# Recurrence with feed-forward on one core: another layout for a, another place for its decay, and a new order

## The chip, the cores and the metric

The kernel runs on one core of one Trainium2 chip. The metric is device time in microseconds. A run of the kernel before took 263.14 us in the median of three (261.58, 263.14, 263.40).

## The reference, cut to what matters

Four batches of eight heads run a recurrence over 768 steps with a 40 x 40 state each. Its output, as 3,072 tokens of 320 features, goes through a feed-forward layer with 2,048 hidden units and a squared relu.

```
for t in range(S):
    y[:, :, t] = einsum('bhd,bhde->bhe', rt, state)
    Sa = einsum('bhde,bhe->bhd', state, at)
    state = state * wt[:, :, None, :] - einsum('bhd,bhe->bhde', Sa, bt) \
            + einsum('bhd,bhe->bhde', vt, kt)
...
h = x @ w_in;  g = maximum(h, 0) ** 2;  out = g @ w_out
```

## The kernel before, in words

The 768 steps are cut into twelve chunks of 64. Within a chunk the recurrence is written as matrix products: w's running products G (the decay from the chunk's start, "the gate") scale k and b by 1/G and a by G, two triangular 64 x 64 products per head stand in for the steps inside the chunk, and a state STb is handed from chunk to chunk. Heads are packed in pairs (two times 40 features in 128 rows, padded to 64) and batches in two halves g of the array's rows, so most matmuls run in a part of the TensorE array: row-tiled (64 x 128), column-tiled (128 x 64), or both (64 x 64). The feed-forward and the sums over steps with UTX run on the whole array.

`load(c)` issues the six inputs of chunk c on SP's queue, two DMAs each. w, k, b, a and v are laid with the step on the partition, so each piece of memory that is read is one head's 40 features of one step, 160 bytes. r alone is laid in eight-step rows: a partition holds eight steps of a head pair's member, 320 values, 1,280 bytes in a piece (`rv`, line 409). An output store has 1,280-byte rows too. Weights go over POOL's queue: WIN in four parts of 256 KB, WOUT in four of 320 KB, WLAST (the last 64 of the 320 input features) in two DMAs of 128 KB.

`prep(c)` makes the chunk's operands. ln of w; hi and lo (its bfloat16 split); ci (matmuls with UTI, inclusive sums of ln w over the steps, for k and b) and ei (exp of minus that, iG); cx (matmuls with UTX, exclusive sums) and ex (exp, Gex); cg (16 matmuls with SEL that have two columns each, line 462: the chunk's whole decay, with the feature on the partition) and eg (exp, gL). mulKB multiplies k and b by iG in two halves; mulA multiplies a by Gex; castR and castV make bfloat16 of r and v. TK, TA and TR are transposes on TensorE into PSUM; tK, tA and tR copy them out (lines 350 and 355 are the copies of VectorE and ScalarE), a's and r's into the two halves of AR. EN is the first triangle (mask mEN, line 556).

`rec(c)` runs AS, EV, NU (with u0 and u1), and S with s, which multiplies the new state by gL while it leaves PSUM (line 648). `read(c)` runs TV, the second triangle CX, RS and Y, y and yd (times Gex, line 718) and the transposes XT. `ffn(c)` works in four quarters u of the hidden units: F (eight whole-array matmuls with WIN, features 0 to 255), FL (four row-tiled ones with WLAST, features 256 to 319, into the same PSUM pair), f (relu, line 772), q (the square, in place, on VectorE line 778 or GpSimd line 780), then O (eight matmuls with WOUT per quarter) and o, the copy out, and st, the store on SP.

PSUM is used as four tiles of a pair of banks; the digit behind PE in the order says which. The order of the instructions of all engines together is written out by hand as one text, ORDER (line 87), whose entries say engine, operation, chunk and part; each engine runs its own entries in that order. A planner's costs (`c_act`, `c_dve`, `pe`) stand in the code, but only ORDER decides. Buffers of raw inputs have two turns, of gates three (NG), of KB and VU three.

Of the kernel before, what the change touches and what calls it, by code (L numbers as in the profile page):

```python
# [91 lines left out]
castV 0 g0; POOL castV 0 g1; PE2 TR 0; DVE mEN 0 g1; ACT tR 0 g0; ACT ex 1; DVE hi 2; PE0 EV 0; SP
ldr 1; DVE lo 2; ACT u0 0; PE3 cx 2; PE NU 0; PE cg 2; ACT u1 0 g0; SP ldv 1; ACT tR 0 g1; DVE
mulKB 1 h0; POOL mulKB 1 h1; ACT u1 0 g1; PE2 S 0 g0; SP ldw 3; ACT ex 2; PE S 0 g1; ACT eg 2; DVE
s 0 q1; PE0 TK 1; POOL mulA 1; DVE s 0 q0; SP ldb 2; ACT castR 1; POOL win3; PE3 TA 1; ACT tK 1;
PE2 TV 0; DVE tA 1; DVE tV 0; PE3 ci 2 h1; SP ldv 2; ACT castV 1 g0; PE0 EN 1 g0; PE2 EN 1 g1; ACT
eg 1; DVE mEN 1 g0; ACT ei 2 h1; PE1 ci 2 h0; ACT ei 2 h0; PE3 CX 0 g1; DVE mEN 1 g1; POOL castV 1
g1; PE0 AS 1; ACT ln 3; POOL win1; PE EV 1; DVE hi 3; DVE mCX 0 g1; PE1 CX 0 g0; ACT u0 1; SP ldk
2; PE2 TR 1; ACT tR 1 g1; PE NU 1; DVE mCX 0 g0; ACT u1 1 g0; DVE tR 1 g0; PE3 Y 0; ACT u1 1 g1;
POOL lo 3; PE1 TS 0; DVE y 0; PE2 TV 1; ACT tS 0; DVE yd 0; PE0 SC 1; DVE tV 1; PE S 1 g0; SP lda  # L100
2; PE3 XT 0; POOL castV 2 g1; PE1 CX 1 g0; PE2 CX 1 g1; DVE xt 0; POOL castV 2 g0; PE S 1 g1; DVE
mCX 1 g0; PE3 RS 1; POOL wlast; SP ldr 3; DVE mCX 1 g1; PE1 cx 3; DVE s 1 q0; PE Y 1; POOL win0;
PE2 ci 3 h0; DVE mulKB 2 h1; PE cg 3; DVE yd 1; DVE y 1; ACT ex 3; SP ldr 2; ACT eg 3; DVE s 1 q1;
PE3 ci 3 h1; PE1 XT 1; ACT ei 3 h1; POOL win2; DVE xt 1; PE0 F 0 u3; DVE mulKB 2 h0; DVE mulA 2;
PE FL 0 u3; SP ldk 4; PE3 TS 1; PE1 TK 2; ACT castR 3; POOL wout0; DVE tK 2; ACT ei 3 h0; ACT f 0
u3; PE2 TR 3; PE1 F 0 u0; SP ldk 3; ACT tR 3 g0; ACT tR 3 g1; PE0 F 1 u0; ACT tS 1; PE FL 1 u0; PE
FL 0 u0; PE2 TA 2; ACT f 1 u0; POOL castR 2; PE3 F 0 u1; DVE tA 2; POOL wout2; ACT f 0 u0; PE0 EN
2 g0; PE2 F 0 u2; DVE mEN 2 g0; SP lda 3; PE FL 0 u2; PE FL 0 u1; DVE q 0 u0; PE1 EN 2 g1; ACT f 0
u2; PE0 F 1 u3; DVE mEN 2 g1; ACT f 0 u1; PE2 AS 2; PE EV 2; POOL wout1; PE FL 1 u3; ACT u0 2; PE1
TR 2; ACT f 1 u3; PE NU 2; PE3 F 1 u1; ACT tR 2 g0; SP ldb 3; DVE q 1 u3; ACT u1 2 g0; PE0 F 1 u2;  # L110
DVE q 0 u3; ACT tR 2 g1; DVE q 0 u2; ACT u1 2 g1; PE FL 1 u1; PE FL 1 u2; DVE q 0 u1; ACT f 1 u1;
PE1 TV 2; POOL wout3; DVE q 1 u0; PE2 O 0 u0; ACT f 1 u2; DVE tV 2; PE3 RS 2; SP ldw 4; DVE q 1
u2; PE0 CX 2 g0; PE1 CX 2 g1; DVE mCX 2 g0; DVE mCX 2 g1; PE O 0 u1; DVE mulA 3; DVE q 1 u1; PE O
0 u2; SP ldv 3; PE0 SC 2; PE S 2 g0; PE Y 2; PE S 2 g1; DVE y 2; PE1 O 1 u0; SP lda 4; DVE s 2 q0;
PE O 1 u1; DVE yd 2; DVE s 2 q1; PE O 0 u3; DVE mulKB 3 h1; SP ldb 4; DVE mulKB 3 h0; PE O 1 u2;
ACT o 0; ACT ln 4; PE3 XT 2; PE0 TA 3; ACT hi 4; PE2 TK 3; DVE xt 2; SP ldw 5; PE O 1 u3; DVE tK
3; POOL castV 3 g1; PE3 F 2 u0; POOL lo 4; DVE tA 3; ACT o 1; ACT castV 3 g0; PE2 EN 3 g1; SP st
0; PE0 EN 3 g0; PE FL 2 u0; DVE mEN 3 g1; PE1 F 2 u2; ACT f 2 u0; DVE mEN 3 g0; PE FL 2 u2; PE2 TS
2; ACT f 2 u2; PE3 AS 3; SP st 1; DVE tS 2; PE EV 3; DVE q 2 u0; PE0 ci 4 h0; ACT u0 3; PE1 ci 4
h1; SP ldv 4; PE2 SC 3; ACT ei 4 h0; PE NU 3; ACT ei 4 h1; PE0 cx 4; ACT u1 3 g0; SP ldr 4; DVE  # L120
mulKB 4 h1; PE cg 4; ACT u1 3 g1; DVE mulKB 4 h0; PE1 F 2 u1; ACT ex 4; ACT eg 4; PE FL 2 u1; ACT
ln 5; DVE mulA 4; PE S 3 g0; SP ldw 6; PE S 3 g1; ACT f 2 u1; POOL hi 5; PE3 TA 4; DVE s 3 q1; PE0
TK 4; POOL lo 5; PE1 TV 3; DVE tA 4; SP ldr 5; ACT tK 4; DVE s 3 q0; PE3 F 2 u3; DVE tV 3; PE2 ci
5 h0; POOL castV 4 g1; PE0 EN 4 g0; SP ldk 5; ACT ei 5 h0; PE FL 2 u3; DVE mEN 4 g0; PE1 EN 4 g1;
POOL castR 4; ACT f 2 u3; PE2 cx 5; SP ldb 5; POOL q 2 u1; PE cg 5; DVE mEN 4 g1; ACT castV 4 g0;
PE0 ci 5 h1; PE3 CX 3 g0; ACT ei 5 h1; PE1 AS 4; DVE mCX 3 g0; PE EV 4; ACT eg 5; ACT ex 5; SP lda
5; PE0 O 2 u0; ACT u0 4; DVE q 2 u2; PE NU 4; PE2 TR 4; ACT u1 4 g0; PE3 CX 3 g1; SP ldv 5; PE O 2
u1; DVE mCX 3 g1; ACT u1 4 g1; ACT tR 4 g0; PE1 RS 3; DVE tR 4 g1; ACT ln 6; PE3 SC 4; PE S 4 g0;
DVE q 2 u3; PE S 4 g1; ACT hi 6; SP ldw 7; PE Y 3; DVE s 4 q0; PE O 2 u2; POOL lo 6; DVE y 3; PE O
2 u3; DVE s 4 q1; POOL castR 5; SP ldb 6; DVE yd 3; DVE mulKB 5 h0; POOL mulKB 5 h1; PE2 XT 3; ACT  # L130
o 2; PE3 TR 5; PE1 TV 4; DVE xt 3; ACT tR 5 g1; PE0 ci 6 h0; DVE tV 4; PE2 F 3 u1; ACT ei 6 h0; SP
ldk 6; POOL mulA 5; ACT tR 5 g0; PE0 ci 6 h1; PE1 CX 4 g0; PE FL 3 u1; ACT ei 6 h1; DVE mCX 4 g0;
PE3 F 3 u3; ACT f 3 u1; PE0 TA 5; SP lda 6; PE1 TS 4; POOL q 3 u1; DVE tA 5; PE2 TS 3; DVE tS 4;
PE FL 3 u3; PE0 TK 5; ACT f 3 u3; DVE tS 3; PE1 F 3 u0; POOL castV 5 g1; SP st 2; DVE tK 5; PE FL
3 u0; PE3 CX 4 g1; ACT f 3 u0; PE2 F 3 u2; DVE mCX 4 g1; ACT ln 7; PE FL 3 u2; PE0 EN 5 g1; PE1 EN
5 g0; ACT f 3 u2; SP ldw 8; DVE mEN 5 g1; PE3 cx 6; PE cg 6; DVE mEN 5 g0; SP ldv 6; PE2 AS 5; ACT
eg 6; POOL hi 7; ACT castV 5 g0; PE0 RS 4; PE Y 4; DVE q 3 u0; POOL mulKB 6 h1; ACT ex 6; PE EV 5;
DVE y 4; PE1 O 3 u0; ACT u0 5; DVE mulKB 6 h0; SP lda 7; POOL mulA 6; PE NU 5; DVE yd 4; PE O 3
u1; DVE q 3 u2; ACT u1 5 g0; ACT u1 5 g1; PE3 TK 6; POOL lo 7; PE0 TA 6; PE2 TV 5; ACT tK 6; DVE
tA 6; PE O 3 u2; DVE tV 5; PE0 cx 7; ACT ln 8; DVE q 3 u3; PE3 CX 5 g1; PE2 XT 4; DVE mCX 5 g1; PE  # L140
O 3 u3; ACT xt 4; PE2 ci 7 h1; ACT o 3; PE3 EN 6 g1; PE cg 7; ACT ei 7 h1; DVE mEN 6 g1; SP st 3;
PE1 EN 6 g0; ACT eg 7; ACT ex 7; PE2 ci 7 h0; DVE mEN 6 g0; PE3 SC 5; SP ldk 7; ACT castV 6 g0; PE
S 5 g0; POOL mulA 7; PE S 5 g1; ACT ei 7 h0; PE0 CX 5 g0; PE1 F 4 u0; DVE mCX 5 g0; SP ldb 7; POOL
castV 6 g1; PE2 F 4 u3; DVE s 5 q0; POOL hi 8; SP ldr 7; PE FL 4 u3; DVE s 5 q1; PE FL 4 u0; POOL
lo 8; ACT f 4 u3; PE0 RS 5; PE Y 5; SP lda 8; PE3 AS 6; ACT f 4 u0; DVE yd 5; PE EV 6; DVE y 5;
PE2 TS 5; SP ldv 7; ACT u0 6; PE1 XT 5; DVE tS 5; PE0 F 4 u1; ACT xt 5; PE FL 4 u1; DVE mulKB 7
h0; POOL mulKB 7 h1; PE2 TA 7; ACT f 4 u1; PE NU 6; SP ldw 9; DVE tA 7; PE1 F 4 u2; ACT u1 6 g0;
DVE q 4 u1; ACT u1 6 g1; PE0 ci 8 h1; POOL castR 7; PE2 TK 7; ACT ei 8 h1; DVE q 4 u0; PE3 ci 8
h0; SP ldr 6; PE FL 4 u2; ACT ei 8 h0; PE0 F 5 u3; DVE tK 7; ACT f 4 u2; PE3 F 5 u0; DVE q 4 u2;
PE FL 5 u3; SP ldb 8; PE1 TV 6; ACT f 5 u3; POOL castV 7 g1; PE2 SC 6; DVE tV 6; PE S 6 g0; SP ldk  # L150
8; PE S 6 g1; POOL q 4 u3; PE0 EN 7 g0; PE FL 5 u0; DVE s 6 q0; PE1 cx 8; ACT f 5 u0; PE cg 8; DVE
mEN 7 g0; PE3 F 5 u2; SP ldb 9; ACT eg 8; ACT ex 8; DVE s 6 q1; POOL castR 6; ACT castV 7 g0; PE
FL 5 u2; PE0 EN 7 g1; POOL mulA 8; PE1 TR 7; ACT f 5 u2; DVE mEN 7 g1; PE2 O 4 u0; SP ldw 10; ACT
tR 7 g0; ACT tR 7 g1; PE3 TS 6; PE0 TR 6; PE1 AS 7; PE EV 7; PE O 4 u1; SP ldv 8; ACT u0 7; DVE
mulKB 8 h0; ACT ln 9; PE O 4 u2; ACT tR 6 g1; DVE tR 6 g0; POOL hi 9; DVE tS 6; POOL mulKB 8 h1;
PE NU 7; PE0 CX 6 g1; ACT u1 7 g0; PE3 CX 6 g0; PE O 4 u3; DVE mCX 6 g0; POOL lo 9; ACT u1 7 g1;
PE1 F 5 u1; DVE mCX 6 g1; ACT o 4; POOL q 5 u0; PE3 TA 8; SP st 4; PE FL 5 u1; PE2 ci 9 h1; DVE tA
# [723 lines left out]
```

## Time and profile before

| | us |
|---|---|
| median of three runs | 263.14 |
| the profiled execution's own time | 260.79 |
| its span, first to last instruction | 258.80 |
| TensorE matmul in flight | 226.8 |
| VectorE busy | 189.0 |
| ScalarE busy | 152.7 |
| GpSimd busy | 96.9 |

The profile is of one execution. A busy share is a mean over the span; stages with different limits are told apart by windows. Matmuls overlap, so their start-to-start distance, and not their mean duration, is what one costs in a dense stretch.

### The profile page before, as it was taken

Reading aid. Unit: us, or ns where it says so; the run is one execution under the profiler, and the core shown is the slowest. Engines: PE = TensorE matmul, PEld = TensorE weight load, DVE = VectorE, ACT = ScalarE, POOL = GpSimd, SP = SyncE. Lnnn points to the kernel's source line nnn. Section 1 sums busy time; section 2 is a strip of 40 time slices with the busy share of each in tenths; the row PEclk is TensorE's granted clock in tenths of the full one; section 3 lists DMA queues with packets and bytes.
Section 4 is the critical chain, followed back from the end, with each engine's and each line's share of the span. In section 5 each row is a group of like instructions: output and inputs, shape, how many; then the busy total and the mean of one; then the engine's idle time right before and its main releaser. Section 6 shows DMA issues by size and latency. Waiting matters only on the chain.

```text
span 258.8 us, 12193 instructions
## 1 busy us (share of the span) xinstructions
PE 226.8 (88%) x5608; PEld 175.3 (68%) x5608; DVE 189.0 (73%) x230; ACT 152.7 (59%) x203; POOL 96.9 (37%) x91
## 2 busy tenths in 40 slices
...
GB/s 110 191 167 175 133 151 159 215 152 165 131 144 179 167 134 148 167 147 7 61 185 144 154 131 149 178 171 151 198 135 4 5 3 54 56 3 3 51 23 78
DMA packets 135506, 30.92 MB, mean 119 GB/s; under 512 B 125728, under 2 KB 135456, under 8 KB 135456
## 3 DMA queue, kind: packets, MB, share of 16 engines
q1 hardware_dynamic: 131712, 27.54, 60.2%
q0 software_dynamic: 3744, 2.62, 7.2%
...
q14 instruction: 7, 0.06, 0.1%
...
## 4 chain that ended last, share of the span: by engine, by line
PE 56%; DVE 18%; DMA 7%; ACT 6%; SPq 6%; issue 4%; POOL 1%; DVEq 0%; ACTq 0%; POOLq 0%
PE pb L369 49%; PE pb L373 7%; DVE EN L556 4%; DMA raw_r<-in_r_dram 3%; DMA raw_w<-in_w_dram 2%; DVE CX L556 2%; DVE STb L648 2%; DMA raw_kb<-in_b_dram 1%; SPq L405 1%; ACT VU L355 1%; DVE AR L350 1%; DVE VUT L350 1%; DVE G L778 1%; SPq L392 1%; ACT AR L355 1%
## 5 line engine op out<-in xcount | busy, mean ns | idle before, releaser
L772 ACT ACTIVATE G<-pb 128x1024 bf16<-128x1024 f32 x46 | 46.1, 1022 | 24.1 <-PE pb L369 23.9
L369 PE MATMUL pb<-WOUT,G 128*128 128x320 bf16 x384 | 57.4, 300 | 0.5 <-DVE G L778 0.4
L369 PE MATMUL pb<-XT,WIN 128*128 128x256 bf16 x384 | 49.2, 276 | 2.2 <-DVE XT L350 1.2
L780 POOL TENSOR_TENSOR G<-G 128x1024 bf16<-128x1024 bf16 x16 | 30.6, 1919 | 42.4 <-ACT G L772 42.4
L369 PEld LDWEIGHTS <-G 128*128 128x128 bf16 x384 | 35.2, 98 | 14.9 <-issue 0.6
L369 PEld LDWEIGHTS <-WIN 128*128 128x128 bf16 x384 | 35.9, 98 | 8.8 <-issue 3.4
L778 DVE TENSOR_TENSOR G<-G 128x1024 bf16<-128x1024 bf16 x32 | 30.6, 975 | 8.7 <-ACT G L772 8.7
L556 DVE TENSOR_TENSOR CX<-pb,MSK 128x1024 bf16<-128x1024 f32 x24 | 28.8, 1219 | 6.2 <-PE pb L369 5.7
L556 DVE TENSOR_TENSOR EN<-pb,MSK 128x1024 bf16<-128x1024 f32 x24 | 28.6, 1217 | 3.2 <-PE pb L369 3.2
L365 DVE TENSOR_TENSOR KB<-raw_kb,iG 128x640 bf16<-128x640 f32 x15 | 14.2, 960 | 11.1 <-ACT iG L444 4.9
L355 ACT ACTIVATE osb<-pb 128x640 f32<-128x640 f32 x12 | 8.5, 704 | 22.9 <-PE pb L369 22.9
L648 DVE TENSOR_TENSOR STb<-pb,gL 64x640 bf16<-64x640 f32 x22 | 18.0, 818 | 4.8 <-PE pb L369 4.4
L355 ACT ACTIVATE VU<-pb 64x640 bf16<-64x640 f32 x23 | 16.0, 697 | 8.4 <-PE pb L369 6.1
L363 POOL TENSOR_TENSOR KB<-raw_kb,iG 128x640 bf16<-128x640 f32 x9 | 15.1, 1681 | 15.5 <-ACT iG L444 5.8
L359 POOL CAST VU<-raw_v 64x640 bf16<-64x640 f32 x14 | 10.0, 721 | 28.6 <-DMA raw_v<-in_v_dram 28.5
L444 ACT ACTIVATE iG<-pb 128x640 f32<-128x640 f32 x24 | 16.4, 702 | 6.7 <-PE pb L369 2.2
L363 POOL TENSOR_TENSOR lo<-lnW,hi 128x640 bf16<-128x640 f32 x8 | 11.7, 1468 | 22.1 <-DMA raw_v<-in_v_dram 7.1
L369 PEld LDWEIGHTS <-EN 64*64 64x64 bf16 x768 | 15.2, 113 | 6.7 <-issue 4.4
L369 PE MATMUL pb<-XT,WLAST 64*128 64x256 bf16 x192 | 17.6, 274 | 0.0
L350 DVE COPY AR<-pb 128x1024 bf16<-128x1024 bf16 (+1 forms) x17 | 11.7, 687 | 6.4 <-PE pb L373 4.0
L355 ACT ACTIVATE AR<-pb 128x512 bf16<-128x512 bf16 x19 | 11.0, 595 | 7.6 <-PE pb L373 7.5
L718 DVE TENSOR_TENSOR Yb<-pb,Gex 128x640 bf16<-128x640 f32 (+1 forms) x24 | 12.6, 549 | 3.1 <-PE pb L369 3.0
...
## 6 DMA issues: line engine op xcount, KB each, us to landing
...
```

The costliest lines, as they stand in the source:

```text
L350: lambda: nc.vector.tensor_copy(out=o_(), in_=i_())))
L355: alts.append(("ACT", c_act(n), lambda: nc.scalar.activation(out=o_(), in_=i_(), func=ACTF.Copy, scale=1.0 if scale is None else scale)))
L363: return [("POOL", 40 + 2.35 * n, lambda: nc.gpsimd.tensor_tensor(out=o_(), in0=a_(), in1=b_(), op=op)), ("DVE", c_dve(n), lambda: nc.vect ...
L365: ("DVE", c_dve(n), lambda: nc.vector.tensor_tensor(out=o_(), in0=a_(), in1=b_(), op=op))]
L369: return lambda: nc.tensor.matmul(out=o_(), lhsT=l_(), rhs=r_(), start=start, stop=stop, skip_group_check=True)
L373: return lambda: nc.tensor.transpose(out=o_(), in_=i_(), identity=IDb[rows(g), :])
L444: ew(f"ei {c} h{jh}", [("ACT", c_act(2 * n), lambda hb=hb, jh=jh: nc.scalar.activation(out=iG[0][:].rearrange("p (g j) e -> p g (j e)", g= ...
L556: evac(f"m{nm} {c} g{g}", lambda s, n: [("DVE", c_dve(n), lambda: nc.vector.tensor_tensor(out=dst[q2][:, g, s].rearrange("p q i t -> p (q ...
L648: ew(f"s {c} q{q}", [("DVE", c_dve(2 * n), lambda q=q: nc.vector.tensor_tensor(out=STb[q2][rows(q), :, q, 0:D], in0=slot(hs, FP32)[rows(q) ...
L772: ("ACT", c_act(1024), lambda gb=gb, hf=hf: nc.scalar.activation(out=gb, in_=slot(hf, FP32)[:], func=ACTF.Relu)),
L778: ("DVE", 690, lambda gv=gv: nc.vector.tensor_tensor(out=gv, in0=gv, in1=gv, op=ALU.mult)),
L780: ("POOL", 1900, lambda gv=gv: nc.gpsimd.tensor_tensor(out=gv, in0=gv, in1=gv, op=ALU.mult))],
```

## The change

- a is loaded like r, in eight-step rows; raw_a has r's shape. castA (GpSimd or ScalarE) makes it bfloat16, and TA transposes it as TR does, without waiting for the gate.
- mulA, SEL, cg and eg are gone. cf, 32 row-tiled matmuls per chunk, makes the running sums of ln w with the feature on the partition; ef takes their exp into GT, 64 steps and a leading 1, 65 columns per head pair. tA, in two halves on VectorE, multiplies the transposed a by GT while it leaves PSUM; s takes the chunk's whole decay from GT's last column.
- Rings of gates (Gex, GT) have two turns, not three.
- In quarters 1 and 3 of the feed-forward FL comes first and opens the PSUM pair, F closes it.
- q can run on ScalarE (Square).
- ORDER is new throughout. By its count of entries: mulKB on GpSimd 18 instead of 9 of 24, hi and lo all twelve on GpSimd (7 and 8 before), castR all twelve on GpSimd (7 before), castV 19 instead of 14 of 24 there, castA 11 of 12 there; q 16 each on VectorE, ScalarE and GpSimd (32, 0, 16 before); relus on VectorE 10 instead of 2; u1 on VectorE 7 instead of 1, tR 10 instead of 5, tV 12 instead of 10, tK 7 instead of 8.

```diff
-ORDER = """SP ldw 0; SP ldw 1; SP ldk 0; SP ldb 0; ACT ln 0; POOL hi 0; DVE lo 0; SP ldr 0; PE0 cx 0; PE cg
-0; PE1 ci 0 h0; ACT ex 0; PE2 ci 0 h1; SP lda 0; ACT ei 0 h1; ACT ei 0 h0; SP ldw 2; ACT ln 1; ACT
-hi 1; ACT eg 0; DVE mulKB 0 h0; POOL lo 1; SP ldv 0; DVE mulKB 0 h1; POOL castR 0; SP ldb 1; PE3
...
+ORDER = """SP ldw 0; SP lda 0; SP ldk 0; SP ldb 0; ACT ln 0; SP ldw 1; POOL castA 0; POOL hi 0; PE0 TA 0;
+POOL lo 0; SP ldv 0; PE1 ci 0 h0; PE2 ci 0 h1; ACT ei 0 h0; PE3 cf 0; ACT ei 0 h1; SP ldb 1; PE1
+cx 0; ACT ef 0; DVE mulKB 0 h1; DVE mulKB 0 h0; DVE tA 0 g0; PE2 TK 0; SP lda 1; DVE tA 0 g1; ACT
...
-    raw_a = buf("raw_a", [128, NJ, D], FP32, NA)
+    raw_a = buf("raw_a", [128, 2, 8 * D], FP32, NA)
...
-    NG = 3
+    NG = 2
     Gex = buf("Gex", [128, NJ, D], FP32, NG)
-    gL = buf("gL", [128, NJ], FP32, NG)
+    GT = buf("GT", [128, NJ, L + 1], FP32, NG)
...
+    for x in GT:
+        nc.vector.memset(x[:, :, 0:1], 1.0)
...
+        for nm, x, ring in (("a", a, raw_a), ("r", r, raw_r)):
+            xv = x[:, :, t0, :].rearrange("b (p q) (k i) e -> q (b p) k (i e)", q=2, i=8)
+
+            def go(xv=xv, ring=ring):
+                for q in range(2):
+                    nc.sync.dma_start(out=ring[c % 2][:, q, :], in_=xv[q])
...
-        pe(f"cg {c}", "D", 2, ms, reads=[("hi",), ("lo",)], writes=[hx])
...
+        hf = ("A", "f", c)
+        ms = []
+        for p in range(NP):
+            for x in (h_, l_):
+                for g in range(2):
+                    ms.append(mm(
+                        lambda p=p, g=g: slot(hf, FP32)[:, g, L * p:L * p + L],
+                        lambda x=x, p=p, g=g: x[rows(g), 2 * p:2 * p + 2, :].rearrange(
+                            "p h e -> p (h e)"),
+                        lambda g=g: UTI[rows(g), 0:L], x is h_ and p == 0, x is l_))
+        pe(f"cf {c}", "R", L, ms, reads=[("hi",), ("lo",)], writes=[hf], alloc=[hf])
+        ew(f"ef {c}", [("ACT", c_act(1024), lambda: nc.scalar.activation(
+            out=GT[q3][:, :, 1:L + 1].rearrange("p (g m) t -> p g m t", g=2),
+            in_=slot(hf, FP32)[:].rearrange("p g (m t) -> p g m t", t=L), func=ACTF.Exp))],
+           reads=[hf], writes=[("GT", q3)], free=[hf])
...
-        ew(f"mulA {c}", mul_alts(lambda: tA[q2][:, :, 0:D], lambda: raw_a[c % NA][:],
-                                 lambda: Gex[q3][:], 640),
-           reads=[("raw", "a", c % NA), ("Gex", q3)], writes=[("tA", q2)])
...
-        ew(f"tA {c}", copy_alts(
-            lambda: AR[q2][:, 0].rearrange("p g j t -> p g (j t)"),
-            lambda: slot(ha, BF16)[:, :, 0:512], 1024, True),
-           reads=[ha], writes=[("AR", q2)], free=[ha])
...
+        for g in range(2):
+            ew(f"tA {c} g{g}", [("DVE", c_dve(512), lambda g=g: nc.vector.tensor_tensor(
+                out=steps(AR[q2][:, 0, g]), in0=turned(ha, g),
+                in1=steps(GT[q3][:, NP * g:NP * g + NP, 0:L]), op=ALU.mult))],
+               reads=[ha, ("GT", q3)], writes=[("AR", q2, g)], free=[ha])
...
-                    in1=gL[c % NG][rows(q), :].rearrange("p (j o) -> p j o", o=1).broadcast_to(
-                        [64, NJ, D]), op=ALU.mult))],
+                    in1=GT[c % NG][rows(q), :, L:L + 1].broadcast_to([64, NJ, D]),
+                    op=ALU.mult))],
...
+            tail = u % 2 == 1
...
+            for x in (1, 0) if tail else (0, 1):
+                if x:
+                    pe(f"FL {c} u{u}", "R", NT, ml, **last)
+                else:
+                    pe(f"F {c} u{u}", "D", NT, ms, **wide)
...
+                ("ACT", c_act(1024), lambda gv=gv: nc.scalar.activation(
+                    out=gv, in_=gv, func=ACTF.Square))],
```

## Rows read from the trace of the kernel before

**Rows 1.** The page, part 1: busy us of each engine, share, instructions.
```profile
PE 226.8 (88%) x5608; PEld 175.3 (68%) x5608; DVE 189.0 (73%) x230; ACT 152.7 (59%) x203; POOL 96.9 (37%) x91
```

**Rows 2.** Windows: length, busy us of five engines, granted clock, DMA share, GB/s.
```profile
10.00:30.00 20.00, 15.07 (x344) 11.04 (x341) 11.63 (x14) 13.36 (x20) 8.67 (x8) 1.00 1.14 163
30.00:50.00 20.00, 14.89 (x456) 11.92 (x451) 16.50 (x21) 9.47 (x16) 6.21 (x8) 0.84 1.08 174
50.00:70.00 20.00, 17.89 (x398) 14.19 (x394) 12.39 (x15) 12.46 (x16) 2.89 (x4) 0.99 1.05 154
70.00:100.00 30.00, 29.29 (x797) 22.69 (x794) 24.28 (x30) 20.92 (x29) 7.69 (x8) 1.00 0.83 156
100.00:130.00 30.00, 27.64 (x735) 21.18 (x734) 27.51 (x29) 18.47 (x26) 17.48 (x14) 1.00 0.55 103
...
210.00:250.00 40.00, 40.00 (x782) 30.45 (x780) 26.07 (x31) 19.58 (x22) 7.98 (x4) 1.00 0.11 27
```

**Rows 3.** The page, part 3: DMA queues of SP (q1) and POOL (q0).
```profile
q1 hardware_dynamic: 131712, 27.54, 60.2%
q0 software_dynamic: 3744, 2.62, 7.2%
```

**Rows 4.** DMA queues in 205 to 250 us.
```profile
q1 hardware_dynamic: 864, 0.98, 9.2%
```

**Rows 5.** The chain of waits in 24 to 62 us: start, us, what.
```profile
26.81 6.32 DMA raw_w<-in_w_dram
```

**Rows 6.** Timeline of TensorE, 100 to 125 us: start, us, line, operation, tiles, count.
```profile
99.75 1.93 PE L369 MATMUL pb<-WOUT,G 128*128 128x320 bf16 x13
101.62 0.65 PE L373 MATMUL pb<-IDb,Yb 64*128 64x64 bf16 x12
...
113.06 0.17 PE L369 MATMUL pb<-SEL,hi 128*128 128x2 bf16 x1
...
113.53 0.48 PE L369 MATMUL pb<-STb,AR 128*64 128x80 bf16 x16
...
118.36 1.26 PE L369 MATMUL pb<-WOUT,G 128*128 128x320 bf16 x8
119.55 0.64 PE L373 MATMUL pb<-IDb,KB 64*128 64x64 bf16 x32
120.03 0.40 PE L373 MATMUL pb<-IDb,tA 64*128 64x64 bf16 x16
```

**Rows 7.** Groups by line and form: busy us, mean ns, idle before, releasers.
```profile
L772 ACT ACTIVATE G<-pb 128x1024 bf16<-128x1024 f32 x46 | 46.1, 1022 | 24.1 <-PE pb L369 23.9
L778 DVE TENSOR_TENSOR G<-G 128x1024 bf16<-128x1024 bf16 x32 | 30.6, 975 | 8.7 <-ACT G L772 8.7
L363 POOL TENSOR_TENSOR KB<-raw_kb,iG 128x640 bf16<-128x640 f32 x9 | 15.1, 1681 | 15.5 <-ACT iG L444 5.8 <-DMA raw_kb<-in_k_dram 5.4 <-DMA raw_kb<-in_b_dram 4.3
L365 DVE TENSOR_TENSOR KB<-raw_kb,iG 128x640 bf16<-128x640 f32 x15 | 14.2, 960 | 11.1 <-ACT iG L444 4.9 <-DMA raw_kb<-in_k_dram 4.4 <-ACT G L772 1.8
L363 POOL TENSOR_TENSOR lo<-lnW,hi 128x640 bf16<-128x640 f32 x8 | 11.7, 1468 | 22.1 <-DMA raw_v<-in_v_dram 7.1 <-ACT gL L470 6.1 <-DVE hi L350 4.7
L350 DVE COPY AR<-pb 128x1024 bf16<-128x1024 bf16 x12 | 8.3, 688 | 4.2 <-PE pb L373 4.0
L359 POOL CAST tR<-raw_r 128x640 bf16<-128x640 f32 x7 | 5.9, 844 | 9.4 <-DMA raw_r<-in_r_dram 9.3
L365 DVE TENSOR_TENSOR tA<-raw_a,Gex 128x640 bf16<-128x640 f32 x6 | 4.9, 818 | 0.8 <-ACT Gex L466 0.8
L350 DVE COPY AR<-pb 128x512 bf16<-128x512 bf16 x5 | 3.4, 687 | 2.2 <-ACT AR L355 2.1
L470 ACT ACTIVATE gL<-pb 128x16 f32<-128x16 f32 x12 | 2.2, 185 | 4.4 <-PE pb L369 4.4
L261 ACT ACT_TABLE_LOAD x1 | 1.3, 1283 | 0.8 <-PEq L865 0.8
```

**Rows 8.** The tile G: duration in ns, min/median/max; first and last start.
```profile
L778 DVE TENSOR_TENSOR G<-G x32: 670/684/3314, 57.4 to 249.4; 128x1024 bf16<-128x1024 bf16 x32
```

More of the change, by code (lines that the diff above doesn't have):

```diff
@@ L92 @@
[L92 to L157, printed above, removed]
```

274 lines of the change are left out of this document (157 added, 117 removed).

## The prediction

> **What bounds the kernel now.** First the busy shares [rows 1]: TensorE has work in flight for 226.8 of 258.8 us, VectorE for 189.0, ScalarE for 152.7, GpSimd for 96.9. The average hides two regimes, so the windows come next [rows 2]. From 210 to 250 us TensorE is busy without a gap, and from 70 to 100 us for 29.29 of 30. From 10 to 70 us it is busy for only 47.85 of 60 us, and in 30 to 50 us at a mean granted clock of 0.84, that is, part of it at 1.2 GHz, the lower level. The same 60 us have a DMA share of 1.05 to 1.14; from 70 us on it is below 0.9. So there is an opening of some 70 us in which transfers set the pace, and behind it about 185 us in which TensorE does. The chain of waits agrees: its largest single piece in the opening is a load of w that takes 6.32 us to land [rows 5].
>
> The price of a load follows from the queues. All loads and stores by SP take 60.2% of 258.8 us on 16 engines, 155.8 us [rows 3]. In 205 to 250 us SP moves three stores and nothing else: 768 of its 864 packets, and 9.2% of 45 us, so 4.14 us or 1.38 us for each store of 256 rows of 1,280 bytes [rows 4]. With r's twelve loads, which have the same rows, at the same price, 24 transfers make 33.1 us; the other sixty (w, k, b, a, v, in pieces of 160 bytes) share 122.7 us, 2.04 us each. The ten weight transfers take 7.2%, 18.6 us, which by size is 1.86 us for a WIN part or for both of WLAST and 2.33 us for a WOUT part [rows 3].
>
> **Lighter a.** In r's layout an a load should cost r's price, 1.38 instead of 2.04 us: 0.66 us less, 7.9 us over twelve. Bounds: nothing gained, if the reads of long rows cost more than the stores from which I priced them, and 0.8 us each if they cost less. Past 70 us the queue has slack, so only what falls into the opening counts: a 0 to a 3 lie before the last WOUT in both orders, 2.6 us.
>
> **Order of the transfers.** I add up the prices of all that stands ahead in the two orders, weights included. Before, the last of chunk 2's w, k, b, a is a 2: 16 loads at 2.04, 2 r at 1.38, 2 WIN at 1.86, together 39.1 us of transfer. After, it is again a 2: 12 at 2.04 and 5 (three a, two r) at 1.38, 31.4 us. For chunk 1 the sums are 21.8 (a 1) and 17.0 (k 1). For chunk 3 they are 62.6 (b 3: 20 at 2.04, 4 r, 5 parts at 1.86, 3 at 2.33) and 47.7 (k 3: 15 at 2.04, 7 at 1.38, 4 parts at 1.86). The last WOUT hardly moves, 64.9 and 65.7. On SP's queue a 0 passes w 1, k 0, b 0, r 0, v 0 no longer waits for w 2, and r 0 and w 1 go back; POOL issues WLAST ahead of WIN now, so the first hidden block is not held by it. TensorE thus has chunk 2's triangles some 8 us of transfer earlier and chunk 3's 15 us earlier, while the second matrix of the feed-forward can begin no sooner. What is that worth? At least the 2.6 us of the lighter loads; at most chunk 2's 7.7 us, because the elementwise engines and the weights then set the pace. I take 5, the middle.
>
> **TensorE.** The 16 two-column matmuls of cg go: from the first to the next block 0.47 us with one change of tile shape [rows 6]. That change is priced by two runs of output matmuls before one: 13 take 1.87 us and 8 take 1.19 us to the next start, so 0.136 us each and 0.10 us for the change [rows 6]. cg is then 0.37 us, 4.4 us over twelve chunks. The 32 half-row matmuls of cf have the shape of TK's 32, which take 0.48 us [rows 6]: 5.8 us. Running the last features first in every second quarter puts row-tiled blocks of two quarters next to each other; counted over the whole order, changes of shape fall from 192 to 179, 1.3 us. Sum: 5.8 - 4.4 - 1.3, nothing. cf also takes a PSUM pair of its own, of four, until ef has read it, about 1.0 us later.
>
> **VectorE.** Off it: six mulA at 0.818, twelve copies tA at 0.688, nine of fifteen mulKB at 0.960, sixteen of 32 squares at 0.975: 37.4 us. Onto it: 24 halves of tA that multiply by the gate, at the 0.687 of a half of the same permuted PSUM tile, 16.5 us [rows 7], and some twenty reliefs of ScalarE (eight relus, six u1, five tR, a net one of tK and tV), which at the 0.975 of a square are 20 us. It stays near 189, and four lo and two hi leave besides. The two tA halves stand 1.4 us in the path to EN where a copy of 0.7 stood, but mulKB, TK and tK run beside them from the same lo, and the wait of TA for the gate is gone.
>
> **ScalarE.** eg at 0.185 becomes ef over 1,024 columns, at the 1.022 of a relu: 10.0 us over twelve. Sixteen squares, also priced at 1.022, are 16.4 us. Eight relus, five tR, five casts of v, five of r, six u1 and three hi leave, 32 instructions between the 0.687 of a half and the 1.022 of a relu, 22 to 33 us. Even again; its idle time of over 100 us [rows 1] covers the rest, and in a stretch without idle time ef costs 0.84 a chunk. The ring of gates goes from three to two, so ex of chunk c now waits for yd of chunk c - 2, with relus and casts queued behind it. In six of ten chunks ex stands seven entries or fewer behind that yd; at about a VectorE instruction (0.975) each that is 0 to 6 us. I take none, because nothing but y needs ex now; the bound goes into the range.
>
> **GpSimd.** 26 more casts (castA, castR, castV, hi) at the 0.844 of r's cast, four more lo at 1.468, nine more mulKB at 1.681, six mulA less at about the same 1.681 [rows 7]: 22 + 5.9 + 15.1 - 10.1, 33 us more, about 130 in all, half of the span. What it costs is the length of a chunk's preparation: mulKB on it takes 1.681 where VectorE takes 0.960. Loads that come earlier by 5 to 15 us cover that in the opening, two chunks of look-ahead later.
>
> **A shared port.** Squares on VectorE take 0.684 us in the median, but one took 3.3 and the mean is 0.975 [rows 7, 8]: 9 us of waiting over 32. VectorE instructions with two SBUF operands (squares, mulKB, mulA, lo) fall from 57 to 22, GpSimd's rise in number. I credit 1 us between 70 and 250 us, where VectorE is busy for 27.51 of 30 us in the worst stretch [rows 2]; bounds are 0 and 3. The Trainium skill (SBUF — State Buffer, "SBUF: two separate sides") says that the two engines take their common port as an exclusive lock, and that the loser blocks for the whole instruction. By that, GpSimd's extra 33 us would speak against the change; the one long square agrees with the lock, and whether more GpSimd or fewer two-operand instructions wins no row shows.
>
> **Sum.** The profiled execution took 260.79 us, span 258.80 and 1.99 around it; the median of the runs, 263.14, is 2.35 above. Opening -5, TensorE 0, port -1: -6, so 254.8 on the profiled basis and 257 on the median's.
>
> **Rivals.**
> (a) The opening is worth more: chunk 2's whole 7.7 us, the 3 us of the port, and half of the 3.2 us that a clock of 0.84 over 20 us takes [rows 2]. 263 - 7.7 - 3 - 1.6 is 251.
> (b) The loads come earlier for nothing: TensorE's work after 70 us has no gaps to give, and the weights, which are as late as before (65.7 against 64.9 us), set when the feed-forward starts. Then nothing but the port is left: 262. For it speaks the gapless 210 to 250 us [rows 2]; against it, that TensorE could do chunk 3's triangles in the gaps of 10 to 70 us.
> (c) GpSimd becomes the late engine. Place: lo, castA, castR, the two mulKB and a square in one queue; whatever is issued behind a late square waits for it, and TK waits for KB. Price: nine mulKB at 0.72 more, 6.5 us, and four lo at 1.468 put on the path, 5.9 us; with the 5 gained in the opening back off, 263 + 12.4 - 5 is about 270. It decides once the keys' transposes wait for GpSimd in most chunks. In the trace TensorE's waits on GpSimd are rare, and GpSimd is idle for over 160 us [rows 1], which speaks against it.
> (d) The square is not in ScalarE's loaded table. The trace has one table load of 1.283 us for all of Ln, Exp, Relu and Copy [rows 7]. If each of sixteen squares needed one there and one back, 41 us would fall on ScalarE; a third to all of it on the path gives 275 to 300. The Trainium skill (ScalarE: Activation LUTs, "Table sets: the hidden batching unit") names relu, copy, identity and abs as held by every set, and not square; with its 2.66 us per switch it would be 85 us. No row has a square on ScalarE.
>
> **Chances.** Forecast 0.46, (a) 0.19, (b) 0.20, (c) 0.12, (d) 0.03. About 1% either way (2.6 us) is what a measurement can tell, as the runs of before spread over 1.8 us. Faster is the forecast and (a): 0.65; the same is (b), 0.20; slower is (c) and (d), 0.15. The range leaves out (d), most of (c) and the better third of (a), 0.03 + 0.10 + 0.06: 249.5 to 265.5.
>
> **What would show it.** Right: packets of SP's queue down by some 21,500 to about 110,000, and its share down by 7 to 8 us; TensorE busy for 50 us or more in 10 to 70 us; EN of chunk 2 some 5 to 8 us earlier; GpSimd near 130 us; tA halves at 0.69, ef and squares at 1.0. Wrong: DMA share still above 1 up to 70 us with the same gaps in TensorE (b), idle TensorE released by GpSimd's KB or lo (c), more than one table load (d). My 5 us is wrong if the opening's gaps turn out to be released by VectorE and ScalarE and not by landings.

## The result and the profile after

The changed kernel takes 254.43 us in the median (251.41 to 258.50, four runs), the kernel before 262.36 (261.04 to 263.40) beside it: a ratio of 0.969 [0.962, 0.976]. Predicted were 257.0 us, 249.5 to 265.5. The first profile of the changed kernel is of its longest run, so the one shown is a second, from the run *new_again*: its own time is 253.11 us, 7.7 us under the 260.79 of the profiled execution of before. Medians here are over all runs, while ratios leave out runs over 1.5% longer than the fastest of their kernel (seven of the ten with the heavy a throughout, and in the table below the executions of that kernel and of the one with one square moved).

The page of *new_again*: busy time by engine, then the two DMA queues.
```profile
PE 225.1 (90%) x5800; PEld 175.4 (70%) x5800; DVE 183.5 (73%) x224; ACT 153.1 (61%) x187; POOL 123.4 (49%) x124
...
q1 hardware_dynamic: 110208, 27.54, 58.2%
q0 software_dynamic: 3744, 2.62, 7.5%
```
Against [rows 1, 3]: SP's packets are 110,208, as forecast, and their time is 58.2% of 251.4 us, 146.3 instead of 155.8. GpSimd has 26.5 us more, VectorE 5.5 less.

Windows of *new_again*: length, busy us of PE, PEld, DVE, ACT and POOL, granted clock, DMA share, GB/s.
```profile
10.00:30.00 20.00, 15.74 (x424) 11.86 (x421) 14.07 (x16) 12.50 (x17) 7.56 (x9) 0.87 1.05 165
30.00:50.00 20.00, 13.86 (x486) 11.09 (x484) 15.24 (x18) 10.13 (x15) 10.99 (x14) 0.87 1.02 181
50.00:70.00 20.00, 19.30 (x470) 15.13 (x471) 14.33 (x20) 15.12 (x17) 8.16 (x10) 0.91 1.14 175
...
100.00:130.00 30.00, 29.96 (x869) 23.83 (x868) 25.43 (x30) 21.00 (x25) 19.84 (x18) 1.00 0.85 162
130.00:160.00 30.00, 29.88 (x822) 23.37 (x821) 25.60 (x29) 19.31 (x25) 18.30 (x17) 1.00 0.74 142
160.00:190.00 30.00, 29.10 (x772) 22.97 (x771) 21.55 (x27) 22.30 (x29) 17.79 (x16) 1.00 0.71 145
190.00:210.00 20.00, 19.80 (x571) 15.56 (x571) 15.64 (x18) 12.15 (x14) 12.59 (x9) 1.00 0.08 20
```
The same view of before, for the stretches that [rows 2] leave out.
```profile
130.00:160.00 30.00, 28.64 (x832) 22.52 (x832) 22.01 (x26) 19.87 (x27) 18.23 (x13) 1.00 0.83 151
160.00:190.00 30.00, 29.80 (x756) 23.67 (x752) 25.03 (x30) 21.66 (x28) 14.87 (x12) 1.00 0.86 168
190.00:210.00 20.00, 17.00 (x510) 13.49 (x502) 16.79 (x17) 13.25 (x19) 9.99 (x7) 1.00 0.20 34
```
In 10 to 70 us, where I had put the gain, TensorE is busy for 48.9 us instead of 47.85, with the DMA share above 1 as before; 50 us or more was my sign of being right. In 100 to 210 us it stands idle for 1.3 us instead of 6.9 (with 27.64 of 30 in [rows 2]), which is 5.7 of the 7.4 us between the two spans. That is the place of most of the gain. What it waited for there says it again: engine, line, releaser, us in total, times, longest. First before, then *new_again*.
```profile
PE pb L369 <- issue: 2.1, 4, 1.3
PE pb L369 <- DVE XT L350: 1.2, 1, 1.2
PE pb L373 <- DVE tA L365: 1.1, 1, 1.1
PE pb L373 <- DVE VUT L350: 0.6, 1, 0.6
PE pb L373 <- POOL KB L363: 0.5, 1, 0.5
PE pb L369 <- DVE G L778: 0.4, 1, 0.4
PE pb L369 <- DVE Sb L350: 0.3, 1, 0.3
```
```profile
PE pb L375 <- issue: 0.4, 1, 0.4
PE pb L371 <- ACT G L784: 0.2, 1, 0.2
PE pb L371 <- DVE Yb L713: 0.2, 1, 0.2
PE pb L371 <- issue: 0.2, 1, 0.2
```
6.2 us of waits have become 1.0. Of the 4.1 us before that have a releaser, 3.6 had VectorE.

**When TensorE was how far.** The two orders do their work in different sequence, so no single instruction marks the same point in both. I added up TensorE's work matmul by matmul, each at its price in a dense run (0.135 us for 320 columns, half-row ones in pairs, 0.10 for a change of shape): 205.2 us of work before, 204.6 after. The table says when 65 us of it were done, and how long the stretch from there to 203 us took, in a profiled execution of each kernel that keeps its order, a few entries aside. They are introduced below. An entry is good to about 1 us, a difference within one order to 0.2 and one between the two orders to 0.5, as the sum depends on what the small shapes are taken to cost.

| kernel | 65 us done at | from there to 203 us done |
|---|---|---|
| before | 100.4 | 151.0 |
| before, one square moved | 102.1 | 152.5 |
| before, 13 squares moved | 104.0 | 154.0 |
| before, ten mulKB moved | 101.4 | 157.3 |
| before, lighter a | 98.2 | 152.1 |
| changed (*new_again*) | 100.2 | 144.4 |
| changed, b of chunk 2 earlier | 100.8 | 144.9 |
| changed, squares back | 101.0 | 147.3 |
| changed, ten mulKB back | 103.4 | 147.6 |
| changed, last features last | 101.5 | 147.0 |
| changed, heavy a from chunk 5 | 104.7 | 148.6 |
| changed, heavy a throughout | 104.6 | 152.0 |

The opening ends at the same time in both orders, 100.4 to 104.0 in four executions of the old with a's old load (mean 102.0) and 100.2 to 104.7 in six of the new with the light a up to there (mean 101.9). The first profile of the changed kernel, which is not in the table, is at about 104.7, with 145.4 behind it. Executions with the same instructions up to 70 us differ by 4.5 us in it (*new_again* and the heavy a from chunk 5), so one pair of traces prices it no finer than that; by this scatter the two means would show a gain of 5 us and not one of 2 (an estimate). The stretch behind it is 6.6 us shorter.

The costs of the new operations in *new_again*, groups by line and form: busy us, mean ns, idle before and its releasers.
```profile
L365 POOL TENSOR_TENSOR KB<-raw_kb,iG 128x640 bf16<-128x640 f32 x18 | 28.6, 1603 | 33.5 <-ACT iG L441 17.6 <-DMA raw_kb<-in_k_dram 10.3 <-DMA raw_kb<-in_b_dram 4.5
L784 ACT ACTIVATE G<-G 128x1024 bf16<-128x1024 bf16 x16 | 16.6, 1051 | 0.1
L780 DVE TENSOR_TENSOR G<-G 128x1024 bf16<-128x1024 bf16 x16 | 15.9, 1004 | 0.0
L526 DVE TENSOR_TENSOR AR<-pb,GT 128x512 bf16<-128x512 bf16 x24 | 15.6, 686 | 2.3 <-ACT GT L470 1.6 <-PE pb L375 0.5
L470 ACT ACTIVATE GT<-pb 128x1024 f32<-128x1024 f32 x12 | 12.3, 1021 | 1.6 <-PE pb L371 1.2 <-DVE EN L551 0.2
L776 DVE TENSOR_SCALAR G<-pb 128x1024 bf16<-128x1024 f32 x10 | 12.2, 1220 | 6.0 <-PE pb L371 6.0
L367 DVE TENSOR_TENSOR KB<-raw_kb,iG 128x640 bf16<-128x640 f32 x6 | 4.8, 822 | 5.1 <-ACT iG L441 3.3 <-ACT Gex L454 1.4 <-issue 0.4
L261 ACT ACT_TABLE_LOAD x1 | 1.3, 1283 | 0.8 <-PEq L869 0.8
```

### The profile page after: what moved, and what is told of

It reads as the page before. It is cut to its first block, busy times and chain, and to the rows that moved or that the text cites. A ratio compares the mean times of both kernels' runs of the same rounds, so it can differ in the third digit from the quotient of the medians.

```text
span 256.8 us, 12605 instructions
## 1 busy us (share of the span) xinstructions
PE 227.0 (88%) x5800; PEld 176.4 (69%) x5800; DVE 183.8 (72%) x224; ACT 153.5 (60%) x187; POOL 123.5 (48%) x124
## 3 DMA queue, kind: packets, MB, share of 16 engines
q1 hardware_dynamic: 110208, 27.54, 57.0%
## 4 chain that ended last, share of the span: by engine, by line
PE 59%; DMA 10%; POOL 10%; issue 6%; DVE 5%; SPq 4%; ACT 4%; POOLq 0%; ACTq 0%; DVEq 0%
PE pb L371 52%; PE pb L375 7%; POOL KB L365 4%; DMA raw_kb<-in_k_dram 4%; DMA raw_kb<-in_b_dram 3%; DMA raw_v<-in_v_dram 2%; DMA raw_a<-in_a_dram 2%; POOL G L782 2%; SPq L394 1%; SPq L410 1%; POOL lo L365 1%; POOL VU L361 1%; POOL hi L361 1%; DVE EN L551 1%; SPq L401 1%
## 5 line engine op out<-in xcount | busy, mean ns | idle before, releaser
L774 ACT ACTIVATE G<-pb 128x1024 bf16<-128x1024 f32 x38 | 38.6, 1024 | 23.7 <-PE pb L371 23.5
L365 POOL TENSOR_TENSOR KB<-raw_kb,iG 128x640 bf16<-128x640 f32 x18 | 28.6, 1600 | 36.9 <-ACT iG L441 16.7
L643 DVE TENSOR_TENSOR STb<-pb,GT 64x640 bf16<-64x640 f32 x22 | 18.1, 821 | 3.1 <-PE pb L371 2.5
L361 POOL CAST hi<-lnW 128x640 bf16<-128x640 f32 x12 | 9.1, 755 | 22.3 <-ACT lnW L419 19.9
L526 DVE TENSOR_TENSOR AR<-pb,GT 128x512 bf16<-128x512 bf16 x24 | 15.6, 685 | 2.8 <-PE pb L375 1.9
L352 DVE COPY VUT<-pb 128x2048 bf16<-128x2048 bf16 x12 | 14.6, 1216 | 3.7 <-PE pb L375 3.6
L365 POOL TENSOR_TENSOR lo<-lnW,hi 128x640 bf16<-128x640 f32 x12 | 16.8, 1396 | 0.8
L361 POOL CAST tA<-raw_a 128x640 bf16<-128x640 f32 x11 | 8.3, 758 | 17.9 <-DMA raw_a<-in_a_dram 17.7
L784 ACT ACTIVATE G<-G 128x1024 bf16<-128x1024 bf16 x16 | 16.6, 1050 | 0.1
L776 DVE TENSOR_SCALAR G<-pb 128x1024 bf16<-128x1024 f32 x10 | 12.2, 1219 | 6.0 <-PE pb L371 6.0
```

Source lines behind the costliest of these rows:

```text
L352: lambda: nc.vector.tensor_copy(out=o_(), in_=i_())))
L361: lambda: nc.gpsimd.tensor_copy(out=o_(), in_=i_())))
L365: return [("POOL", 40 + 2.35 * n, lambda: nc.gpsimd.tensor_tensor(out=o_(), in0=a_(), in1=b_(), op=op)), ("DVE", c_dve(n), lambda: nc.vect ...
L526: ew(f"tA {c} g{g}", [("DVE", c_dve(512), lambda g=g: nc.vector.tensor_tensor(out=steps(AR[q2][:, 0, g]), in0=turned(ha, g), in1=steps(GT[ ...
L643: ew(f"s {c} q{q}", [("DVE", c_dve(2 * n), lambda q=q: nc.vector.tensor_tensor(out=STb[q2][rows(q), :, q, 0:D], in0=slot(hs, FP32)[rows(q) ...
L774: ("ACT", c_act(1024), lambda gb=gb, hf=hf: nc.scalar.activation(out=gb, in_=slot(hf, FP32)[:], func=ACTF.Relu)),
```

## The experiments

Ratios are to the kernel before on the same chip, with 95% intervals; 0.01 is 2.6 us. T is the theory that transfers in the opening bring the gain (the prediction's), L that the late part and its elementwise work do, R that an order of instructions and an order of loads belong together, P that the load on VectorE and its shared port does, S that the order as a whole does.

**The changed kernel again.**

> The changed kernel once more, for a second profile. Theory T (the opening: lighter and earlier transfers give the time): its TensorE reaches the end of the opening ahead of the kernel before, by 3 to 5 us at the first output copies' side of the chain or at the state copies of chunks 3 and 4. Rival L (the late part gives it: VectorE's squares no longer wait for GpSimd, and the stretch from 190 to 210 us has no gaps): at 100 us it is not ahead of the kernel before, and the 8 us come between 100 us and the end. Both: ratio 0.96 to 0.976.

Measured: 254.88 us, 0.971 [0.963, 0.979]. The tables above are from it.

**The lighter a alone, in the kernel before.**
```diff
-                for g in range(2):
-                    nc.sync.dma_start(out=ring[c % len(ring)][rows(g)], in_=half(x, g))
+                for q in range(2):
+                    nc.sync.dma_start(out=ring[c % len(ring)][:].rearrange(
+                        "p (q i) e -> p q (i e)", q=2)[:, q, :], in_=xv[q])
```


> The kernel before, in which only a's loads are laid in rows of 1,280 bytes (the values of a then sit in other places than the arithmetic expects, so its output is not the reference's; the instructions are the same). T: 2.6 us faster by the four loads in the opening, ratio 0.99, at most 0.985. L: nothing, ratio 0.996 to 1.004. In the trace SP's queue falls by 7 to 8 us of transfer.

Measured: 260.46 us, 0.993 [0.989, 0.997]: 1.8 us, nearer to the 2.6 of the prediction (T) than to the nothing of L. In the table this execution is early at 65 us (98.2) and a little slower than before from there on. That would put the gain into the opening, but 2.2 us is within the scatter of it.

**The heavy a back in the changed kernel**, in all twelve loads, and then in the seven from chunk 5 on, which SP issues behind the first output store (there the condition is `nm == "a" and c >= 5`).
```diff
-                    nc.sync.dma_start(out=ring[c % 2][:, q, :], in_=xv[q])
+                    if nm == "a":
+                        nc.sync.dma_start(out=ring[c % 2][rows(q)].rearrange(
+                            "p s (i e) -> p (s i) e", e=D), in_=half(x, q))
+                    else:
+                        nc.sync.dma_start(out=ring[c % 2][:, q, :], in_=xv[q])
```


> The changed kernel, in which only a's loads go back to pieces of 160 bytes (values in other places, output not the reference's; the instructions are the same). T: 2.6 us or more slower than the changed kernel, so 0.98 of the kernel before instead of 0.97. L: no difference from the changed kernel, 0.965 to 0.975. In the trace SP's queue rises by 7 to 8 us of transfer.

> The changed kernel with a in 160-byte pieces again from chunk 5 on (seven loads, all issued behind the first output store at 78 us); a of chunks 0 to 4 stays in eight-step rows. The values of a from chunk 5 on land in other places, so the output differs; every instruction and duration but those seven loads stays. With all twelve in pieces the ratio to before was 1.005, or 9 to 11 us more than the changed kernel. As the prediction had it (past 70 us the queue has slack, so only what falls into the opening counts): the seven late ones cost nothing, ratio 0.969, about 254 to 255 us, and the 9 to 11 us belong to a 0 to a 4. Rival L (loads issued behind a store are themselves the path past 70 us): nearly all of it belongs to the late seven, ratio 0.995 to 1.005, 261 to 264 us. Both alike, in the ratio of the counts (five to seven): 260 us, ratio 0.99. If the late seven cost it, TensorE waits for KB or AR between 100 and 210 us with a load of k, b or v ahead of it in the chain, and the first output store still stands at 78 us.

Measured: 265.57 us, 1.005 [0.998, 1.012] for all twelve, 9 us more than the changed kernel (the difference of the ratios); 259.5 us, 0.990 [0.981, 0.998] for the late seven, some 5 us more, to 2 or 3 either way. So "past 70 us the queue has slack" is wrong: the late loads cost about 0.7 us each, and the early five about 4 us together. The chain of waits of the kernel with seven heavy loads shows the way (start, us, what).
```profile
106.38 0.24 SPq L809
...
107.39 0.63 SPq L411
...
111.03 1.84 SPq L394
112.92 5.05 DMA raw_kb<-in_k_dram
...
119.62 0.53 POOL KB L365
```
SP issues the store of chunk 2 (L809) only when ScalarE has made its copy, and behind the store stand, in one queue, a 7 (L411), b 6 and k 6 (L394). GpSimd's mulKB waits for k 6; it starts at 118.12 us, in *new_again* at 111.05 and behind the gate, not behind k 6 (the store is 4.5 us later here already). The DMA share of that stretch is below 1 (0.87 in 100 to 130 us): the queue has idle time on average, and none behind a store. In *new_again* TensorE makes 86.5% of the chain from 104 to 126 us. TensorE's waits in 100 to 210 us, of this kernel:
```profile
PE pb L375 <- POOL KB L365: 1.9, 2, 1.2
PE pb L371 <- ACT G L788: 1.2, 1, 1.2
```
Its window from 100 to 130 us has one thing more, a granted clock of 0.94, where *new_again* has 1.00:
```profile
100.00:130.00 30.00, 27.58 (x680) 20.84 (x672) 20.45 (x25) 17.25 (x20) 17.01 (x14) 0.94 0.87 150
```
In part of it, that is, the clock is at the lower level, 1.2 GHz, which takes up to 1.8 us (0.06 of 30). So of the 4.2 us by which the table has this execution slower behind 65 us, not all is the wait itself.

**The new order of the loads in the kernel before.** All entries of SP in the changed kernel's sequence, each as early as its buffer allows; the other engines' entries stay.
```diff
-SP ldw 0; SP ldw 1; SP ldk 0; SP ldb 0; SP ldr 0; SP lda 0; SP ldw 2; ...
+SP ldw 0; SP lda 0; SP ldk 0; SP ldb 0; SP ldw 1; SP ldv 0; SP ldb 1; ...
```


> The kernel before, with its loads and stores on SP in the sequence of the changed kernel (one load of chunk 8 two places earlier, where that sequence would block), each as early as its buffer allows; all else as before, weights included. T: the inputs of chunks 2 and 3 land 5 to 8 us of transfer earlier and the kernel is 2 to 4 us faster, ratio 0.985 to 0.992. L, or a rival R that says the order of the instructions has to go with the order of the loads: ratio 0.995 or above, for the engines' own queues still take chunk 2's and 3's work in the old places.

Measured: 298.26 us, 1.140 [1.132, 1.147]. Of SP's own waits in it:
```profile
SPq L799 <- ACT osb L353: 77.0, 6, 29.0
SPq L398 <- DVE tA L363: 11.1, 1, 11.1
SPq L403 <- POOL VU L357: 7.8, 1, 7.8
```
L799 is a store, L398 and L403 are loads (a and v) that wait for their buffers. Waits of stores are no fault in themselves, as *new_again* has 80.3 us of the first kind. But a load that the old order needs early now stands behind one whose buffer is freed late. So this order of loads has no worth without the order of instructions that belongs to it, and the sums of transfers that I compared in the prediction priced one queue without the waits in it. What the earlier transfers would bring alone the run doesn't show.

**b of chunk 2 earlier in the changed kernel.** In *new_again* the chain runs through this load in the opening:
```profile
31.12 6.35 DMA raw_kb<-in_b_dram
...
37.63 3.05 POOL KB L365 x2
...
40.73 0.32 PE pb L375 x10
```
```diff
-SP ldk 2; SP ldv 2; SP ldb 2;
+SP ldk 2; SP ldb 2; SP ldv 2;
```


> The changed kernel with the load of chunk 2's b one place earlier on SP, ahead of v of chunk 2. In the changed kernel's second profile the chain of the opening runs through that load (6.35 us to land at 37.5 us) and GpSimd's two mulKB behind it. T (transfers set the pace of the opening): b lands 2 us earlier and the kernel is 0.5 to 2 us faster than the changed one, ratio to the kernel before 0.962 to 0.968. If the opening is held by what comes behind (mulKB, weights), no difference: 0.968 to 0.976.

Measured: 254.03 us, 0.969 [0.963, 0.975], no change. b 2 lands at 33.8 instead of 37.5 us, and EN of chunk 2 starts at 46.4 us in both: a 2 takes its place in the chain. One landing has taken the place of another, so the run doesn't decide between T and its rival.
```profile
34.39 5.94 DMA raw_a<-in_a_dram
```

**ScalarE's squares back on VectorE in the changed kernel.**
```diff
-ACT q 0 u0
+DVE q 0 u0
```
and fifteen more like it.

> The changed kernel with its sixteen ScalarE squares back on VectorE, at their places in the order. Theory P (the time comes from 100 us on, because VectorE has fewer instructions with two SBUF operands, that is, fewer that stand still while GpSimd works, and is nowhere full): sixteen squares at 0.68 to 0.98 us come back on VectorE, 3 to 6 us of it in front of something that TensorE waits for, ratio to the kernel before 0.982 to 0.995. Theory S (VectorE is not it; the order of instructions and loads as a whole is): no difference from the changed kernel, 0.965 to 0.976.

Measured: 258.56 us, 0.984 [0.979, 0.989]: 3.4 us more (0.013).

**Ten mulKB back on VectorE in the changed kernel**, those that the change moved to GpSimd.
```diff
-POOL mulKB 2 h1
+DVE mulKB 2 h1
```


> The changed kernel with ten mulKB on VectorE that the kernel before also had there (GpSimd keeps eight), at their places in the order. P: ten at 0.96 us come back on VectorE, ratio 0.98 to 0.99. Rival (c) of the prediction (GpSimd is late, mulKB's 0.72 us more lie on the path): faster than the changed kernel by 2 to 6 us, 0.95 to 0.963. S: no difference, 0.965 to 0.976.

Measured: 259.95 us, 0.987 [0.983, 0.992]: 4.4 us more, though each takes less time there than the 1,603 ns of GpSimd. VectorE's group of them grows in mean from 822 to 1,009 ns:
```profile
L365 DVE TENSOR_TENSOR KB<-raw_kb,iG 128x640 bf16<-128x640 f32 x16 | 16.0, 1009 | 4.9 <-ACT iG L439 3.3 <-ACT Gex L452 1.5
```
and TensorE's longest wait in 100 to 210 us is for VectorE again:
```profile
PE pb L369 <- DVE Sb L350: 2.1, 1, 2.1
```

**The same two moves in the kernel before**: thirteen squares to ScalarE (those that the change moves there and the old order had on VectorE), ten mulKB to GpSimd, and one square alone, the one of 3.3 us [rows 8], at 200 us.
```diff
-DVE q 0 u0
+ACT q 0 u0
```
```diff
-DVE mulKB 2 h1
+POOL mulKB 2 h1
```
```diff
-DVE q 8 u2
+ACT q 8 u2
```


> The kernel before with thirteen of its VectorE squares on ScalarE, the ones that the changed kernel has there too, at their places in the order. P: VectorE loses 9 to 13 us of work, 1 to 4 us of it in front of TensorE, ratio 0.985 to 0.995. S: nothing, 0.996 to 1.004. Rival (d) of the prediction, a reload of ScalarE's table per square: 1.05 or more.

> The kernel before with ten mulKB on GpSimd instead of VectorE, the ones that the changed kernel has there too, at their places in the order. P: VectorE is relieved of 10 us, above all between 100 and 130 us where it is full; 2 to 4 us faster, ratio 0.985 to 0.993. S, or rival (c) of the prediction: GpSimd takes 1.68 us for each at a place that was planned for 0.83, ratio 1.00 to 1.02.

> The kernel before with a single square (chunk 8, quarter 2) on ScalarE, the one that stood for 3.31 us on VectorE at 200 us while GpSimd worked. P: the 2.6 us above its usual 0.68 come off the path, for the gate multiplication of the last chunk stands right behind it on VectorE and TensorE waits for that: 2 to 2.6 us faster, ratio 0.99 to 0.992, and the gap of TensorE at 203 us is gone. S: the time is taken by the next wait, ratio 0.997 to 1.003.

Measured: 1.012 [1.007, 1.017], 1.020 [1.015, 1.024] and 0.998 [0.994, 1.001]. What costs 3 to 4 us to undo in the new order costs 3 to 5 us to do in the old. The single square should have brought 2 to 2.6 us by P and brought 0.6 (-0.3 to 1.5): taking the longest VectorE instruction off that engine gained next to nothing, as S had it. With the ten mulKB in the old order GpSimd's KB are waited for:
```profile
PE pb L367 <- issue: 2.9, 3, 1.9
PE pb L371 <- POOL KB L361: 1.9, 2, 1.6
```
More than these waits, the clock sets this execution apart. The rows of the granted clock in the two pages, 40 slices of the span, first before, then with the ten mulKB moved:
```profile
PEclk9999988799999999999999999999999999999999
PEclk9999999999999999979997999999997999999998
```
Three times between 100 and 210 us, where before has none, it falls to the lower level, at 116.8 us behind a gap of TensorE of 0.84 us: there eight output matmuls take 2.25 us, and 1.26 at 122.6 us. The windows have 0.94, 0.94, 1.00 and 0.91 for 100 to 130, 130 to 160, 160 to 190 and 190 to 210 us, together up to 5.4 us of the 6.3 that the table has this execution slower. For the thirteen squares no row of the trace names one cause: its waits are spread over eight rows.

**Last features last in all quarters of the changed kernel.** Changes of shape become 213 instead of 179.
```diff
-            tail = u % 2 == 1
+            tail = False
...
-PE2 FL 0 u1; PE F 0 u1;
+PE2 F 0 u1; PE FL 0 u1;
```


> The changed kernel with F ahead of FL in all quarters, the two entries of quarters 1 and 3 exchanged in the order. Both theories: a few more changes of tile shape at 0.10 us each, 1 to 3 us slower than the changed kernel, 0.975 to 0.983. Were a change of shape free where it stands, no difference.

Measured: 258.59 us, 0.988 [0.984, 0.992]: 4.5 us more. 34 changes at 0.10 us are 3.4 of it, and TensorE's work comes out at 207.9 us by the sum above, against 204.6.

## Why the prediction came out

The time, 254.4, is within the range and 2.6 us under the forecast, and the gain, 7.7 us between the two profiled executions, is near the 6 of the sum. That is luck: the largest term of the sum did not come about, and a gain as large came where I had put 1 us.

**Opening, 5 us: failed.** EN of chunk 2 did come earlier, at 46.4 instead of 56.3 us, even more than the 5 to 8 foreseen, and chunk 3's at 68.9 instead of 79.2. It bought nothing that shows: the first output copy comes at 77.3 us instead of 74.7, the second at 87.4 instead of 78.0, and the two means at 65 us of work are 102.0 and 101.9. The new order does other work first, and as much of it. The step that failed is the reading of the DMA share of 1.05 to 1.14 as the bound of the opening, by which inputs that land earlier were worth up to 7.7 us there. The waits of TensorE, which the prediction doesn't show for these 60 us, tell who releases it there; in the kernel before, 10 to 70 us, its longest lines are
```profile
PE pb L373 <- DVE KB L365: 2.6, 2, 2.3
PE pb L373 <- issue: 1.7, 2, 1.3
PE pb L369 <- DVE EN L556: 1.4, 3, 0.7
PE pb L369 <- DVE CX L556: 1.4, 3, 0.7
```
Of the 12.1 us of all its lines, 10.2 are released by VectorE and ScalarE. It is the case that the prediction gave as its own refutation. The landing of w in [rows 5] is 6.3 us of the chain in there, and in the 14 us behind it stand 10 us of elementwise work. That transfers have no part isn't shown by this: the view names the last releaser only, VectorE's mulKB themselves stood idle for 4.4 us until k landed [rows 7], the chain of *new_again* runs through b 2, and the lighter a alone brought the old order 1.8 us. The weights are later too: WOUT's last two parts land at 70.7 and 73.6 us (59.8 and 62.3 before), because GpSimd, which issues them, waits ahead of a mulKB:
```profile
62.96 1.54 POOL L365 TENSOR_TENSOR KB<-raw_kb,iG 128x640 bf16<-128x640 f32 x1 [10.01 <-ACT iG L441]
64.45 0.81 POOL L824 DMA_DIRECT2D WOUT<-in_moe_w_out_dram  x1
```
I had summed the transfers ahead of them and left out the wait of the engine that issues them.

**Lighter a: right in price, wrong in place.** SP's packets take 9.5 us less, 0.79 per load where I took 0.66, at the bound of 0.8. By the Trainium skill (DMA: Bandwidth & Descriptors, "Why small descriptors are slow (HBM only)") a packet costs some three cycles beside one for every 32 bytes, by which 160-byte pieces cost (5 + 3)/5 against (40 + 3)/40, 1.49 times as much per byte (an estimate by that page). The prediction's prices are near that, with 2.04 against 1.38 us, 1.48 [rows 3, 4]; the measured saving says more, 2.04 against 1.25 us, 1.63, and it decides. It is the late seven that I priced at nothing, and they are worth about 5 us in the new order.

**TensorE, 0: right.** 205.2 us of work before, 204.6 after. The order of F and FL, which I gave 1.3 us, is worth more inside the new order (3.4 us by the count, 4.5 measured), as that order would have 213 changes of shape without it and not the 192 of the old.

**VectorE even, the port 1 us: too small.** VectorE has 183.5 us, not 189. What its instructions take over their medians is halved: squares over 684 ns and mulKB over 826 stood for (975 - 684) x 32 and (960 - 826) x 15 ns before [rows 7], 11.3 us, and squares for (1,004 - 682) x 16, 5.2 us, after. That it is the port that they wait for is argued and not shown: no row names it, and the longest of them, taken away alone, was worth 0.6 us. In 100 to 130 us VectorE is busy for 25.43 us instead of 27.51, and 2.3 us of TensorE's gaps are gone there; but in 130 to 160 us, where 1.2 are gone, it is busy for 25.60 instead of 22.01. The moves of squares and mulKB carry 3.4 and 4.4 us in the new order; I had credited 1.

**ScalarE even, GpSimd 130: right**, or nearly, with 153.1 and 123.4. ef takes 1.02 us, a half of tA 0.69, both as taken.

**The rivals.** (d) is refuted: sixteen squares at 1.05 us and one table load. The Trainium skill (ScalarE: Activation LUTs, "Table sets: the hidden batching unit") doesn't list square among what every set holds; the measurement decides, Square runs beside Ln, Exp, Relu and Copy with the table loaded once. (c) is refuted for the new order by the mulKB put back on VectorE: less GpSimd is slower, not faster. (b) is half right: its sign came, the DMA share above 1 with the same gaps, and the opening gained nothing that shows; but there were gaps to take behind 70 us. (a), at 251, is about as far off as the forecast, and for the same wrong reason.

**What stays open.** The parts undone one by one in the new order cost 9, 3.4, 4.4 and 4.5 us, each to 2 or 3 either way, some 21 in all, for a gain of 8; done one by one in the old they bring 1.8 or cost 3 to 5. So their worths don't add, and a share of the 8 us per part can't be given. The early five a loads seem to carry 4 us by the ratios, yet the table shows the opening ending at 104.7 with and 104.6 without them, within its scatter of 4.5 us; which it is stays open. How much of each part's cost is its own wait, and how much the clock that falls behind it, is open too.
